# Column maxima of k: from the third batch on by 32x32 transposes on VectorE and a row through DRAM, instead of eight TensorE transposes, with a new order list

## The chip, the cores and the metric

The kernel runs on one core of one Trainium2 chip. The metric is the device time of one execution in microseconds (us). Three runs of the kernel before gave 468.64, 469.94 and 470.07 us; their median is 469.94 us.

## The reference

Two blocks follow each other: linear attention over 8 batches, 8 heads, 576 positions and head size 64, and a feed-forward block (512 to 1024 to 512) over the 4608 rows that come out of it.

```
q_s = softmax(q) over the head size;  k_s = softmax(k) over the 576 positions
kv  = einsum('bhsd,bhse->bhde', k_s, v);  attn = einsum('bhsd,bhde->bhse', q_s, kv)
x   = attn, as (8*576) rows of 8*64
h   = x @ w_in
sm  = softmax(h) over the 1024;  solu = h * sm
ln  = (solu - mean) / sqrt(var + 1e-6) * g_ln
out = ln @ w_out
```

The softmax of k needs, for each of the 512 columns (head, head size) of a batch, the maximum over its 576 positions. The change is about that maximum.

## The kernel before

**Tiles.** The 4608 rows are cut into 36 row tiles of 128 rows: four per batch and, for every pair of batches, a fifth from the 64 rows that each has left over. A row tile goes through `attend` (x, 16 or 32 small matmuls on TensorE, called PE in the profile), `hidden` (h, 24 matmuls of 128x512 and then the chain of SoLU and layer norm on VectorE, ScalarE and GpSimd: DVE, ACT and POOL) and `project` (o, 24 matmuls of 128x512, one eviction, one store). The operands are split in two float16 parts, and h and o are sums of three products each. The transposed u (uT) is made by a DMA transpose, and up to 12 of these tiles stand ready ahead of o.

**Keys.** `keys(b)` (line 354) works once per batch. k lies as 128 partitions by (8 heads, 4 positions, 64), plus the rest of 64 partitions. VectorE takes maxima over the positions within a partition (khalf, ktop; L365, L367) and of the rest (L370). `ktop` is then 128 partitions by 512 columns, and the maximum over the partitions is missing. `tops_of` (line 336) makes it: four PE transposes of 128x128 (`turned`, L341), a maximum on VectorE (`col`, L344), four more PE transposes of the broadcast `col` (`wide`, L348), which puts the 512 maxima on every partition, and a copy out of PSUM on ScalarE (`kb`, L351). Then follow the subtraction from k (`km`, L376, in two halves of four heads, and `kr`, L381), the exponentials (L378, L383), the product with v on PE (`kv`, L395 and L400), the denominators, a power-of-two scale and the block-diagonal `bd` that x reads.

**Queues.** All DMAs are issued by SyncE (SP): loads of q, k, v and the weights, the DMA transposes, and the stores. SP, like the other engines, takes its instructions strictly in order; one that waits holds what is behind it.

**Order.** Nothing is scheduled by a tool. Each piece of work is a generator, and the string `ORDER` names which generator takes its next step: `K2` is the next step of keys of batch 2, `h3` of hidden of the fourth row tile, `o0` of project of the first, `P` a filler of four matmuls (`warm_up`, L696), `Q`, `V`, `LK`, `LQ`, `R`, `S`, `w`, `y`, `W`, `Z` the loads, the query softmax, the scales and the weights. A suffix `.v` puts a step that may run on several engines on VectorE. So the string sets the order within every engine and, for many steps, the engine.

**Start.** In the first 73 us the weights are read as 64-bit words, converted on VectorE and ScalarE (L258 to L330), and the first tiles of x and h are made between; o can only begin when `wo` is ready.

Of the kernel before, what the change touches and what calls it, by code (L numbers as in the profile page):

```python
# [8 lines left out]
F32 = mybir.dt.float32  # L9
# [5 lines left out]
ALU = mybir.AluOpType  # L15
AX = mybir.AxisListType

P = 128
# [3 lines left out]
WHOLE = 1  # L22
ORDER = (
# [78 lines left out]
def linear_attention_solu_ffn(ctx: ExitStack, tc: tile.TileContext, q, k, v, w_in, w_out, g_ln, out):  # L102
# [7 lines left out]
    nc = tc.nc  # L110
    B, H, S, D = q.shape
    DM, DF = w_in.shape[0], w_out.shape[0]
    NP = H // 2
# [647 lines left out]
```

## Time and profile before

| | |
|---|---|
| three runs | 468.64, 469.94, 470.07 us |
| profiled execution | 468.76 us, of which the span of the instructions is 467.0 us |
| busy over the span | PE 439.9, DVE 349.9, ACT 282.4, POOL 200.0 us |
| granted PE clock | 0.996 of full speed |
| moved by DMA | 74.99 MB |

Times in the profile count from the start of the span. Busy is the union of an engine's instructions; a matmul's recorded duration includes its way through the array, so that matmuls that follow each other overlap in the records and the distance of their starts, not their duration, is what each costs. L and a number is a line of the kernel before. In the lists of order that are quoted below, lines of the changed kernel stand 23 higher in this part of the code, and a number behind a tile's name tells buffers apart.

### The profile page before, as it was taken

What the parts mean: (1) busy time and instruction counts of PE and PEld (TensorE: products, weight loads), DVE (VectorE), ACT (ScalarE), POOL (GpSimd) and SP (SyncE); (2) the same over time, 40 slices, a digit from 0 to 9 for tenths busy, and PEclk for the clock granted to TensorE, in tenths of its full rate; (3) what the DMA queues carried; (4) which work ended last, traced back from release to release, by engine and by line L of the source; (5) the groups of instructions that cost most, each with busy time, mean ns of one, the idle gap of its engine ahead of it and who ended that gap; (6) DMA issues with size and microseconds to landing.
All of it is one profiled execution on the core that took longest, in us unless ns stands there. A gap on an engine that the chain in (4) does not pass through costs nothing.

```text
span 467.0 us, 8294 instructions
## 1 busy us (share of the span) xinstructions
PE 439.9 (94%) x3142; PEld 221.4 (47%) x3142; DVE 349.9 (75%) x620; ACT 282.4 (60%) x469; POOL 200.0 (43%) x286
## 2 busy tenths in 40 slices
PE   0678889999999999999999999999999999999997
PEld 0334344455546454545454455445545445444445
DVE  4989999998987889879789788668877844633500
ACT  1789899777658657466667448654764454522401
POOL 4123966577159356314665322735364421211200
PEclk9989999999999999999999999999999999999999
DMA  8999989589593997598757973869324673232522
GB/s 251 311 316 303 208 190 214 104 215 207 152 237 72 219 231 159 146 193 212 146 126 210 226 141 63 226 146 201 71 67 46 135 163 54 60 70 71 133 63 67
DMA packets 159240, 74.99 MB, mean 161 GB/s; under 512 B 127840, under 2 KB 152672, under 8 KB 159200
## 3 DMA queue, kind: packets, MB, share of 16 engines
q1 hardware_dynamic: 159200, 74.47, 69.0%
q8 instruction: 24, 0.39, 0.4%
q14 instruction: 16, 0.13, 0.1%
HBM read 36.70 MB, written 9.44 MB: 99 GB/s over the span
## 4 chain that ended last, share of the span: by engine, by line
PE 86%; DVE 6%; POOL 3%; ACT 3%; DMA 1%; issue 1%; SPq 0%; POOLq 0%; ACTq 0%; DVEq 0%
PE o L640 40%; PE h L566 36%; PE x L529 3%; PE kv L395 3%; PE warm_up L696 1%; DMA qm<-in_q_dram 1%; PE kv L400 1%; DVE wi L289 1%; DVE qnmx L443 1%; POOL qm L445 1%; PE turned L341 1%; PE wide L348 1%; DVE iw L262 1%; POOL km L376 1%; DVE km L376 0%
## 5 line engine op out<-in xcount | busy, mean ns | idle before, releaser
L640 PE MATMUL o<-wo,uT 128*128 128x512 f16 (+1 forms) x888 | 197.4, 373 | 0.0
L566 PE MATMUL h<-wi,xT 128*128 128x512 f16 x840 | 193.1, 379 | 2.7 <-ACT e L609 2.3
L640 PEld LDWEIGHTS <-uT 128*128 128x128 f16 x888 | 86.2, 98 | 97.8 <-issue 0.3
L566 PEld LDWEIGHTS <-xT 128*128 128x128 f16 x840 | 81.5, 98 | 98.8 <-issue 3.0
L573 DVE TENSOR_REDUCE top<-h 128x1 f32<-128x1024 f32 x36 | 43.9, 1221 | 24.9 <-PE h L566 24.7
L602 DVE SCALAR_TENSOR_TENSOR u<-h,nmu,u 128x1024 f16<-128x1024 f32 x36 | 46.0, 1277 | 16.7 <-ACT u L600 16.5
L609 ACT ACTIVATE e<-h,nmu 128x1024 f32<-128x1024 f32 x36 | 40.1, 1113 | 22.1 <-DVE u L602 22.1
L595 DVE SCALAR_TENSOR_TENSOR h<-h,ph,e 128x1024 f32<-128x1024 f32 x36 | 46.3, 1287 | 5.5 <-POOL ph L592 4.0
L589 POOL TENSOR_TENSOR p<-pi,mone 128x1 f32<-128x1 f32 x36 | 25.9, 718 | 49.5 <-DVE pi L586 42.7
L600 ACT ACTIVATE u<-h,nmu 128x1024 f16<-128x1024 f32 x36 | 40.0, 1112 | 0.8
L579 ACT ACTIVATE e<-h,nm,hs 128x1024 f32<-128x1024 f32 x31 | 37.2, 1201 | 0.7
L597 ACT ACTIVATE nmu<-s 128x1 f32<-128x1 f32 x36 | 7.3, 202 | 49.4 <-DVE h L595 49.3
L445 POOL TENSOR_TENSOR qm<-qm,qnmx 128x1024 f32<-128x1024 f32 (+1 forms) x14 | 25.7, 1844 | 21.7 <-DVE qnmx L443 14.6
L650 ACT ACTIVATE os<-o,rr 128x512 f32<-128x512 f32 (+1 forms) x23 | 15.3, 667 | 31.1 <-PE o L640 24.4
L622 POOL TENSOR_TENSOR r<-var,mhalf 128x1 f32<-128x1 f32 x36 | 24.2, 675 | 22.5 <-DVE var L619 22.0
L461 POOL TENSOR_TENSOR qhl<-qm,qhl 128x1024 f16<-128x1024 f32 (+1 forms) x11 | 22.5, 2041 | 19.4 <-DVE qhl L163 10.3
L575 ACT ACTIVATE nm<-top,hs 128x1 f32<-128x1 f32 x31 | 9.1, 294 | 35.2 <-DVE top L573 35.0
L456 POOL TENSOR_TENSOR qm<-qm,qrec 128x1024 f32<-128x1024 f32 (+1 forms) x11 | 20.7, 1879 | 19.2 <-DVE qrec L454 19.1
L543 DVE SCALAR_TENSOR_TENSOR xT<-x,xT 128x512 f16<-128x512 f32 x35 | 23.6, 683 | 5.2 <-ACT xT L541 5.1
L586 POOL TENSOR_SCALAR pi<-am 128x1 f32<-128x1 f32 x19 | 7.5, 393 | 41.8 <-DVE am L583 41.1
L443 DVE TENSOR_REDUCE qnmx<-qm 128x16 f32<-128x1024 f32 (+1 forms) x17 | 19.3, 1147 | 6.0 <-DMA qm<-in_q_dram 6.0
L541 ACT ACTIVATE xT<-x 128x512 f16<-128x512 f32 x35 | 20.0, 590 | 5.9 <-PE x L529 5.8
(139 smaller groups left out, 547.4 us busy)
## 6 DMA issues: line engine op xcount, KB each, us to landing
v<-in_v_dram SPq DMA_DIRECT2D x32, 256.0 KB, 3.7
out_dram<-os SPq DMA_DIRECT2D x31, 256.0 KB, 3.4
km<-in_k_dram SPq DMA_DIRECT2D x7, 1024.0 KB, 7.1
qm<-in_q_dram SPq DMA_DIRECT2D x7, 1024.0 KB, 6.8
w_in<-in_moe_w_in_dram SPq DMA_DIRECT2D x8, 512.0 KB, 6.9
w_out<-in_moe_w_out_dram SPq DMA_DIRECT2D x8, 512.0 KB, 5.6
out_dram<-os SPq DMA_DIRECT2D x10, 128.0 KB, 2.7
qm<-in_q_dram SPq DMA_DIRECT2D x2, 512.0 KB, 4.4
```

The lines of the kernel that those rows point to most:

```text
L443: nc.vector.tensor_reduce(shaped(nmx), x, axis=AX.X, op=ALU.max, negate=True)
L445: on(nc.gpsimd).tensor_tensor(x, x, wide(nmx), op=ALU.add)
L566: nc.tensor.matmul(h[:, ns], xT[:, t, kc], wi[:, s, kc, ns], start=(i == 0), stop=(i == len(terms) - 1))
L573: nc.vector.tensor_reduce(top, h, axis=AX.X, op=ALU.max, negate=True)
L579: nc.scalar.activation(e, h, AF.Exp, bias=nm, scale=hs, accum_out=z)
L589: nc.gpsimd.tensor_tensor(p, pi, mone, op=ALU.pow)
L595: nc.vector.scalar_tensor_tensor(h, h, ph, e, op0=ALU.mult, op1=ALU.mult, accum_out=s1)
L600: nc.scalar.activation(u[:, 0], h, AF.Identity, bias=nmu)
L602: nc.vector.scalar_tensor_tensor(u[:, 1], h, nmu, u[:, 0], op0=ALU.add, op1=ALU.subtract)
L609: nc.scalar.activation(e, h, AF.Square, bias=nmu, accum_out=s2)
L622: nc.gpsimd.tensor_tensor(r, var, mhalf, op=ALU.pow)
L640: nc.tensor.matmul(o, uT[:, j, f], wo[:, s, f, cols], start=(f == 0 and j == 0 and s == 0), stop=(f == NF - 1 and j == 1))
```

## The change

From the third batch on (`b >= SPREAD`, with `SPREAD = 2`, so for six of eight batches) `tops_of` goes another way:

- VectorE transposes `ktop` in blocks of 32x32 (`blocks`, L343 of the changed kernel) and takes the maximum over each run of 32 (`part`, 128 partitions by 16; L346).
- One PE transpose turns `part` into 16 partitions by 128 (`turned`, L349), and VectorE takes the maximum over the four groups of 32 (`row`, 16 by 32: the 512 maxima; L352).
- SP stores `row` in a DRAM buffer (`line`, 2 KB; L355), and, once that has landed, loads it back with a broadcast to all 128 partitions (`kb`, 256 KB; L359).

The first two batches keep the path of before. `kb` is what it was for the subtraction that follows. x stays in single tiles of 16 matmuls, as before.

The order list is a new one: nearly every item stands elsewhere, and a number of steps changed their engine. Its first line, before and after:

```
-    "LQ0*2 Q0a*2 LK0*3 Q0b.v Q0c.v Q0a.v Q0b V03 K0.v w3 Q0a w3 K0 Q0a.v Q0a K0*2 Q0b V03 Q0c.v*2 V00 w0 "
+    "LQ0*2 Q0a Q0b Q0a LK0 Q0c LK0 K0 Q0a LK0 Q0b Q0b.v V03 Q0a w3 Q0c K0 w3 K0 V03 V00.v Q0a.v Q0a*2 w0 "
```

The rest of the diff:

```
+SPREAD = 2
...
+    hbm = ctx.enter_context(tc.tile_pool(name="hbm", bufs=1, space=bass.MemoryType.DRAM))
...
     def tops_of(top, b):
 
         flat = top.rearrange("p h d -> p (h d)")
+        if b >= SPREAD:
+            blocks = sb.tile([P, NP * P], F32, name=f"blocks{b}", tag="kb", bufs=1)
+            nc.vector.transpose(blocks, flat)
+            yield
+            part = sm.tile([P, NP * 4], F32, name=f"part{b}", tag="part", bufs=1)
+            nc.vector.tensor_reduce(part, blocks.rearrange("p (i r) -> p i r", r=32), axis=AX.X, op=ALU.max)
+            yield
+            turned = ps.tile([NP * 4, P], F32, name=f"turned{b}", tag="att", bufs=3)
+            nc.tensor.transpose(turned, part, ident)
+            yield
+            row = sm.tile([NP * 4, 32], F32, name=f"row{b}", tag="row", bufs=1)
+            nc.vector.tensor_reduce(row, turned.rearrange("p (g r) -> p r g", r=32), axis=AX.X, op=ALU.max)
+            yield
+            line = hbm.tile([NP * 4, 32], F32, name=f"line{b}", tag="line", bufs=2)
+            nc.sync.dma_start(out=line, in_=row)
+            yield
+            kb = sb.tile([P, H, D], F32, name=f"kb{b}", tag="kb", bufs=1)
+            wide = line.rearrange("i r -> (i r)").unsqueeze(0).broadcast_to([P, NP * P])
+            nc.sync.dma_start(out=kb.rearrange("p h d -> p (h d)"), in_=wide)
+            yield kb
+            return
         turned = ps.tile([P, NP, P], F32, name=f"turned{b}", tag="att", bufs=3)
         for i in range(NP):
             nc.tensor.transpose(turned[:, i], flat[:, i * P : (i + 1) * P], ident)
```

146 rows, old and new, of the table ORDER are left out of this document.

## The prediction

> **What bounds the kernel now.** I read the page first, for the busy times and the chain that ended last.
>
> ```profile
> PE 439.9 (94%) x3142; PEld 221.4 (47%) x3142; DVE 349.9 (75%) x620; ACT 282.4 (60%) x469; POOL 200.0 (43%) x286
> PE 86%; DVE 6%; POOL 3%; ACT 3%; DMA 1%; issue 1%; SPq 0%; POOLq 0%; ACTq 0%; DVEq 0%
> ```
>
> PE carries 86% of the chain, so the question is whether what the change takes from PE is paid back somewhere. Next I cut the span at 73.21 us, where the chain begins to consist of PE alone, and asked for the busy times of that long stretch, for what PE waited for in it, and for three pieces of the chain.
>
> ```profile
> 73.21:463.50 390.29, 390.29 (x2734) 196.02 (x2733) 286.67 (x510) 225.74 (x382) 166.83 (x249) 1.00 0.64 143
> PE h L566 <- ACT e L609: 0.4, 1, 0.4
> 77.68 5.18 PE o L640 x24
> 119.78 1.52 PE x L529 x64
> 190.73 1.87 PE kv L395 x64
> ```
>
> The first row gives the stretch, PE's busy time in it and then PE's weight loads, DVE, ACT and POOL. PE is busy all of 390.3 us, and the only wait that the trace lists for it is one of 0.4 us. A matmul of o or h costs 5.18/24 = 0.216 us, one of x 1.52/64 = 0.024, one of kv 1.87/64 = 0.029. DVE has 390.3 - 286.7 = 103.6 us free there. So from 73 us on, a microsecond of PE work less is a microsecond less of span, as long as nobody makes PE wait.
>
> **What is removed from PE.** A group of four transposes, twice per batch, shows in the timeline of batch 7; beside it stands a single transpose of the same kind.
>
> ```profile
> 330.31 0.59 PE L640 MATMUL o<-wo,uT 128*128 128x512 f16 x2
> 330.75 0.60 PE L341 MATMUL turned<-ident,ktop 128*128 128x128 f32 x4
> 331.18 1.46 PE L640 MATMUL o<-wo,uT 128*128 128x512 f16 x6
> 332.48 0.60 PE L348 MATMUL wide<-ident,col 128*128 128x128 f32 x4
> 332.91 1.24 PE L566 MATMUL h<-wi,xT 128*128 128x512 f16 x5
> ...
> 113.46 0.27 PE L173 MATMUL kv<-ident,mx 128*128 128x128 f32 x1
> 113.57 0.38 PE L566 MATMUL h<-wi,xT 128*128 128x512 f16 x1
> ```
>
> Starts count, not durations: `turned` takes PE from 330.75 to 331.18, 0.43 us, `wide` from 332.48 to 332.91, again 0.43; the single one 113.57 - 113.46 = 0.11. The new path keeps one transpose (bounds 0.11, and 0.27 if nothing overlaps it; I take 0.11, since it stands between matmuls as the single one does). Per batch 0.43 + 0.43 - 0.11 = 0.75, for six batches 4.5 us less; with the upper bound 3.5.
>
> The Trainium skill, page "TensorE: Matmul & The Clock Gate", section "Part 4: PE-mode transpose", puts one transpose at about 275 ns in a kernel's context. The records' 0.27 us agree as a duration, but the starts stand 0.11 apart; charged singly, 48 removed and 6 added would give 42 x 0.275 = 11.6 us instead of 4.5.
>
> The lists of order show the place. In both, PE's rows are at batch 2: before, between o of the third row tile and x; `bd` and `uT` are the stationary operands.
>
> ```order
> L640 LDWEIGHTS uT0_2_780
> L640 MATMUL o0_20_1084<-wo_68,uT0_2_780 128x512
> L348 MATMUL wide2_1118<-ident_86,col2_1114 128x128 x4
> L529 LDWEIGHTS bd1_81
> L529 MATMUL x1_2_1132<-qT1_2_1054,bd1_81 64x128
> ```
>
> After, on PE, between h of the sixth row tile and o of the third:
>
> ```order
> L589 LDWEIGHTS xT1_0_968
> L589 MATMUL h1_0_1022<-wi_69,xT1_0_968 128x512
> L349 MATMUL turned2_1076<-ident_88,part2_1070 16x128
> L663 LDWEIGHTS uT0_2_830
> L663 MATMUL o0_20_1078<-wo_70,uT0_2_830 128x512
> ```
>
> Two visits of four have become one visit of one, and PE waits for DVE once per batch instead of twice.
>
> **What is added to VectorE, and taken from ScalarE.**
>
> ```profile
> L344 DVE TENSOR_REDUCE col<-turned 128x4 f32<-128x512 f32 x8 | 5.5, 688 | 1.8 <-PE turned L341 1.8
> L163 DVE COPY vm<-v 128x512 f32<-128x512 f32 x7 | 2.8, 403 | 0.0
> L365 DVE TENSOR_TENSOR khalf<-km 128x512 f32<-128x512 f32 x16 | 12.1, 754 | 0.1
> L176 DVE TENSOR_REDUCE top_kv<-kv 128x1 f32<-128x128 f32 x8 | 2.3, 286 | 2.3 <-PE kv L173 2.3
> L351 ACT COPY kb<-wide 128x512 f32<-128x512 f32 x8 | 4.7, 585 | 8.1 <-PE wide L348 8.1
> ```
>
> No 32x32 transpose is in the trace. Over 128x512 in float32 a copy takes 0.40 us and a two-operand instruction 0.75; I take 0.69, as the one-operand reduction of that size (an estimate). Then `part` 0.69 and `row` 0.29 come, and `col` 0.69 goes: 0.98 more per batch, 5.9 us in six batches. ACT loses 6 x 0.585 = 3.5. All of it lies beside PE work, in an engine with 103.6 us free: I cost it at nothing. If that cover is gone, it is at most those 5.9 us.
>
> **What is added to SP, and the new wait.** SP before, around the stores of the first two o (`os`), the loads of q and v, and the transposes of u:
>
> ```order
> L484 DMA_TRANSPOSE qT1_2_1054<-qhl1_1_994 128x16x128
> L201 DMA qm2_1092<-in_q_dram 128x8x256
> L653 DMA out_0_dram<-os0_10_1037 128x512
> L653 DMA out_0_dram<-os0_00_949 128x512
> L605 DMA_TRANSPOSE uT1_1_1168<-u1_1_1068 128x16x128
> ```
>
> SP after, at the same stores:
>
> ```order
> L507 DMA_TRANSPOSE qT1_2_1105<-qhl1_1_1003 128x16x128
> L355 DMA line2_1107<-row2_1103 16x32
> L676 DMA out_0_dram<-os0_10_1049 128x512
> L359 DMA kb2_1162<-line2_1107 128x512
> L676 DMA out_0_dram<-os0_00_979 128x512
> L209 DMA v3_1_1168<-in_v_dram 128x2x256
> L628 DMA_TRANSPOSE uT1_1_1183<-u1_1_1113 128x16x128
> ```
>
> The load of `kb` waits on SP until `line` has landed; behind it are a store, a load of v for the next batch, and the transposes of u. All three are needed much later (up to 12 uT stand ready for o), so that SP's wait costs nothing by itself. On DVE the first half of km waits for kb, with xT and u of two row tiles behind it, and seven instructions between `row` and it; on POOL kr waits, with the second half of km and the next q subtraction behind it. What may cost is the round trip. The nearest transfers are the stores of an output tile and the loads of v, 256 KB like `kb`; the answers by source line give their time to landing.
>
> ```profile
> DMA to landing us min/median/max: 1.9/3.3/8.3
> DMA to landing us min/median/max: 2.9/3.7/9.4
> ```
>
> The first row is the output stores (L653), the second the loads of v (L207). Round trip T = 3.3 + 3.7 = 7.0 us, bounds 1.9 + 2.9 = 4.8 and 8.3 + 9.4 = 17.7. What else stands between `turned` and the second half of kv:
>
> ```profile
> L376 POOL TENSOR_TENSOR km<-km,kb 128x1024 f32<-128x1024 f32 x8 | 18.9, 2359 | 1.7 <-ACT kb L351 1.5
> L381 POOL TENSOR_TENSOR kr<-kr,kb 64x512 f32<-64x512 f32 x5 | 6.3, 1265 | 2.6 <-ACT kb L351 2.5
> L378 ACT ACTIVATE km<-km 128x1024 f32<-128x1024 f32 x16 | 16.8, 1052 | 1.9 <-POOL km L376 1.0 <-DVE km L376 0.7
> ```
>
> 0.27 (the transpose) + 0.29 (`row`) + T + 1.27 + 2.36 + 1.05 = 5.2 + T. Its cover in batch 2 is what the new list puts on PE behind `turned`: 24 matmuls of o, 32 of x, 24 of h, 48 x 0.216 + 32 x 0.024 = 11.1 us, and the first half of kv, 0.9. So PE waits when T exceeds 6.8 us. Counted likewise, batches 3 to 7 have 14.2, 14.7, 18.6, 18.6 and 25.5 us, and wait from T = 9.9, 10.4, 14.3, 14.3 and 21.2. At 7.0 only batch 2 waits, 0.2 us; `row` also stands behind a 0.7 us reduction on DVE, and I take 0.5 us (bounds 0, and 2.2 at T = 9).
>
> The Trainium skill, page "DMA: Bandwidth & Descriptors", section "Anatomy of one DMA", gives about 2.0 us per transfer plus its bytes at 436 GB/s, for DMAs issued by GpSimd. That would be an estimated 2.0 + 2.6 = 4.6 us, and a wait of 0 instead of 0.5.
>
> **The start.** Two moves of the new list touch the chain there, whose rows are:
>
> ```profile
> 12.44 1.22 DVE qm L445
> 13.66 0.59 DVE ktop L370
> ...
> 32.49 1.02 PE warm_up L696 x4
> 33.52 0.57 PE x L529 x16
> ```
>
> DVE before, at the first batch's maxima:
>
> ```order
> L365 TENSOR_TENSOR khalf0_117<-km0_103 128x512
> L367 TENSOR_TENSOR ktop0_116<-khalf0_117 128x256
> L445 TENSOR_TENSOR qm0_97<-qm0_97,qnmx0_2_110 128x8x128
> L370 TENSOR_TENSOR ktop0_116<-ktop0_116,kr0_106 64x512
> L450 TENSOR_REDUCE qsum0_1_145<-qm0_97 128x8
> ```
>
> DVE after, there:
>
> ```order
> L388 TENSOR_TENSOR khalf0_113<-km0_107 128x512
> L479 TENSOR_TENSOR qm0_99<-qm0_99,qrec0_0_126 128x8x64
> L390 TENSOR_TENSOR ktop0_112<-khalf0_113 128x256
> L393 TENSOR_TENSOR ktop0_112<-ktop0_112,kr0_116 64x512
> L473 TENSOR_REDUCE qsum0_1_153<-qm0_99 128x8
> ```
>
> The q subtraction (L445) has gone to POOL, 1.22 us off the chain; and of the fillers between the first kv and the first x there are three instead of four, 1.02. Together 2.2 us at most. But later in the start three engines are full:
>
> ```profile
> 50.00:60.00 10.00, 8.50 (x53) 3.90 (x53) 9.59 (x15) 9.36 (x14) 9.37 (x8) 1.00 1.04 211
> ```
>
> (DVE 9.59, ACT 9.36, POOL 9.37 of 10 us, DMA share 1.04.) The list has as much ACT work up to there as before, so a lead gained early is mostly lost. I take 0.8 us less; bounds 2.2 less and 1.0 more.
>
> **The sum.** -4.5 - 0.8 + 0.5 = -4.8 us. The profiled execution was 468.76 us (span 467.0 and 1.76 around it), the median of the runs 469.94; the two differ by 1.2, so I set out from their middle, 469.4: 464.6 us. With all bounds of this case: 469.4 - 4.5 - 2.2 = 462.7, and 469.4 - 3.5 + 1.0 + 2.2 = 469.1.
>
> **The rivals.** A difference within 0.3%, 1.4 us, can hardly be told from no change.
>
> *The round trip ends slower.* kb lands late, and the subtractions, on DVE or POOL, hold h's chain behind them while PE stands at kv. It decides where the waits of batches 2, 3 and 4 eat the 5.3 us and 1.4 more: (T - 6.8) + (T - 9.9) + (T - 10.4) = 6.7, T = 11.3 us. At T = 12.5 the waits are 5.7 + 2.6 + 2.1 = 10.4, the time 469.4 - 5.3 + 10.4 = 474.5 us. For it speaks that single landings of 8.3 and 9.4 us exist; against it the medians, and that both would have to be slow together in several batches. 9 in 100.
>
> *The start gives it back.* The new list reaches the dense stretch 4 us later: 469.4 - 4.5 + 4.0 = 468.9 us, no change. For it speaks that three engines are full from 50 to 60 us, so one step in the wrong place is felt; against it the two moves above, and that of DVE's list one L445 and one L461 of the start have gone to POOL, which is idle early. 13 in 100.
>
> *The start gains more,* 3 us instead of 0.8, if both moves carry through and a wait of h for its buffer shrinks: 469.4 - 4.5 - 3.0 = 461.9 us. 5 in 100.
>
> *Every transpose costs its recorded duration.* Then PE is freed of (48 - 6) x 0.27 = 11.3 us: 469.4 - 11.3 = 458.1 us. The starts of rows L341 and L640 speak against it. 3 in 100. It is the page's 275 ns of the Trainium skill taken as a price; the trace disagrees with that reading.
>
> That the change doesn't do what it says can be left out: PE's list after has one `turned` and no `wide` in each batch from 2 on.
>
> **How the numbers follow.** The forecast, 464.6 us, has the remaining 70 in 100. Faster by over 0.3%: 70 + 5 + 3 = 78; within: 13; slower: 9. The range of 461.5 to 469.1 us holds the forecast with its bounds, the better start and the start that gives it back; 12 in 100, the last rival and the slower one, lie outside.
>
> **What would show it.** Right: L349 once per batch at 0.11 us of PE between its neighbours; DVE busy about as before, ACT some 3 us less; PE's waits after 75 us below 1.5 us, the longest at kv of batch 2, for exponentials of km; the dense stretch beginning near 72 us. Wrong: waits of kv for km in three batches or more; `line` and `kb` above 11 us together; a 32x32 transpose well over 0.75 us; the first o matmul later than 77.7 us; or new waits of h for e or xT in the dense stretch, which would mean that the new list, not the new path, decides.

## The result and the profile after

| | before | after |
|---|---|---|
| median of five runs | 468.76 us (468.35 to 470.07) | 472.84 us (472.40 to 474.83) |
| ratio, 95% interval | | 1.0087 (1.0059 to 1.0114) |
| span of the profiled execution | 467.0 us | 470.8 us |
| granted PE clock | 0.996 | 0.989 |

The change makes the kernel slower by 4.1 us, 0.9%; forecast were 4.8 us less. Here and below, a ratio leaves out runs of over 1.5% above the fastest of the same kernel (four of twelve in E4 and in E7), and a median holds all runs. The page of the changed kernel, busy times and chain:

```profile
PE 440.5 (94%) x3096; PEld 218.4 (46%) x3096; DVE 359.0 (76%) x614; ACT 279.2 (59%) x463; POOL 206.9 (44%) x304
PE 66%; DVE 16%; DMA 7%; ACT 5%; issue 3%; POOL 1%; SPq 0%; ACTq 0%; DVEq 0%; POOLq 0%
```

PE's busy time is as before although it has work less, and only 66% of the chain are PE's (86% before). What PE waited for from 73 us on, in us in total, times and longest:

```profile
PE h L589 <- ACT e L632: 2.1, 3, 1.1
PE kv L418 <- ACT km L401: 2.1, 1, 2.1
PE o L663 <- ACT os L673: 1.9, 1, 1.9
PE x L552 <- DMA qT<-qhl: 0.3, 1, 0.3
```

Before, this list had one row of 0.4 us. The operations of the new path itself cost what was forecast; by group (busy, mean ns of one) and, for its two DMAs, by issue (KB, median us to landing):

```profile
L343 DVE STREAM_TRANSPOSE blocks<-ktop 128x512 f32<-128x512 f32 x6 | 4.2, 702 | 0.1
L346 DVE TENSOR_REDUCE part<-blocks 128x16 f32<-128x512 f32 x6 | 4.1, 683 | 0.1
L352 DVE TENSOR_REDUCE row<-turned 16x32 f32<-16x128 f32 x6 | 1.6, 274 | 3.6 <-PE turned L349 3.6
L349 PE MATMUL turned<-ident,part 128*16 128x128 f32 x6 | 1.6, 272 | 0.0
```

```profile
kb<-line SPq DMA_DIRECT2D x6, 256.0 KB, 3.9
line<-row SPq DMA_DIRECT2D x6, 2.0 KB, 2.1
```

The 32x32 transpose takes 0.70 us (forecast 0.69), the round trip 2.1 + 3.9 = 6.0 us (forecast 7.0). These are medians: from the issue of `line` to the landing of `kb` it is 5.2 us in batch 2, 8.5 and 8.7 in batches 3 and 4, and 5.0 to 6.8 in the others; of these six, only batch 2 has a kv that waits. So the loss is not in the path's own rows.

**Where PE stands.** The timeline of PE at the first two o (start, us, what; in brackets the idle time before it and its releaser), of before:

```profile
73.21 4.48 PE L566 MATMUL h<-wi,xT 128*128 128x512 f16 x20 [0.41 <-ACT e L609]
77.52 5.34 PE L640 MATMUL o<-wo,uT 128*128 128x512 f16 x24
82.70 1.03 PE L566 MATMUL h<-wi,xT 128*128 128x512 f16 x4
83.70 4.48 PE L640 MATMUL o<-wo,uT 128*128 128x512 f16 x20
```

And of after:

```profile
73.40 5.34 PE L589 MATMUL h<-wi,xT 128*128 128x512 f16 x24 [0.49 <-ACT e L632]
78.57 5.34 PE L663 MATMUL o<-wo,uT 128*128 128x512 f16 x24
85.79 2.53 PE L663 MATMUL o<-wo,uT 128*128 128x512 f16 x11 [1.88 <-ACT os L673]
```

The first o starts 1.05 us later. Of this, 4 x 0.216 = 0.86 us is work that has only changed places: all 24 matmuls of an h stand ahead of the first o now, where before 20 stood ahead of it and four behind. That h itself begins 0.19 us later. So the new list has the second o directly behind the first, and nothing between them. There is one PSUM buffer of o, and ScalarE empties it only after a u, part of q and an xT: PE waits 1.88 us.

The timeline of after at batch 2, all engines:

```profile
102.34 1.28 DVE L618 SCALAR_TENSOR_TENSOR h<-h,ph,e 128x1024 f32<-128x1024 f32 x1
102.39 1.27 POOL L404 TENSOR_TENSOR kr<-kr,kb 64x512 f32<-64x512 f32 x1
...
103.54 5.37 DVE L399 TENSOR_TENSOR km<-km,kb 128x1024 f32<-128x1024 f32 x1
103.62 2.34 POOL L399 TENSOR_TENSOR km<-km,kb 128x1024 f32<-128x1024 f32 x1
...
105.93 1.89 POOL L468 TENSOR_TENSOR qm<-qm,qnmx 128x1024 f32<-128x1024 f32 x1
...
108.94 1.06 ACT L401 ACTIVATE km<-km 128x1024 f32<-128x1024 f32 x1 [3.88 <-DVE km L399]
...
110.05 2.17 PE L418 MATMUL kv<-vm,km 128*64 128x65 f32 x38 [2.05 <-ACT km L401]
```

kb is there at 102.39, for POOL has begun to subtract it. DVE's half of km takes 5.37 us, 1.21 elsewhere: it begins at 103.54 and ends 1.1 us after POOL's string of kr, km and qm. POOL's own half of km is done at 105.96, in time for kv. The product h (L618), whose first operand lies in PSUM, ran beside kr in its usual 1.28. So PE gets the exponentials of DVE's half 2.05 us late. Right behind, the granted clock falls (0.66, the column after POOL's):

```profile
110.00:115.00 5.00, 4.95 (x84) 4.39 (x85) 3.85 (x9) 4.97 (x8) 2.65 (x5) 0.66 0.63 115
```

5 x 0.34 = 1.7 us of PE work more. The same picture stands at the seventh kv (batch 6), with a factor of one element per partition:

```profile
283.31 1.26 POOL L404 TENSOR_TENSOR kr<-kr,kb 64x512 f32<-64x512 f32 x1
283.38 4.05 DVE L615 TENSOR_TENSOR ph<-p,hs 128x1 f32<-128x1 f32 x1 [0.57 <-POOL p L612]
284.54 0.54 POOL L645 TENSOR_TENSOR r<-var,mhalf 128x1 f32<-128x1 f32 x1
285.05 2.35 POOL L399 TENSOR_TENSOR km<-km,kb 128x1024 f32<-128x1024 f32 x1
...
287.53 1.29 DVE L618 SCALAR_TENSOR_TENSOR h<-h,ph,e 128x1024 f32<-128x1024 f32 x1
...
295.46 1.89 PE L589 MATMUL h<-wi,xT 128*128 128x512 f16 x8 [1.08 <-ACT e L632]
```

`ph` takes 4.05 us instead of 0.15, and PE waits for this chain's e at 295 and again (0.58) at 314 us. Take for every DVE record what it lasts beyond the median of the same operation, tile and shape in the kernel before: the sum is 7.6 us before (the longest 1.3) and 15.9 after, 8.1 of it in these two rows.

The Trainium skill, page "SBUF — State Buffer", section "Who interferes with whom", has the rule: a VectorE instruction with two operands in SBUF reads the second through a port that it shares with GpSimd; against a GpSimd instruction that reads SBUF, whoever issues first has it for the whole instruction, and the other is blocked. The two rows agree, and go further: VectorE did not get in between POOL's instructions either, but waited for up to three of them (kr, km, qm).

### The profile page after: what moved, and what is told of

It reads as the page before. It is cut to its first block, busy times and chain, and to the rows that moved or that the text cites. A ratio compares the mean times of both kernels' runs of the same rounds, so it can differ in the third digit from the quotient of the medians.

```text
span 470.8 us, 8231 instructions
## 1 busy us (share of the span) xinstructions
PE 440.5 (94%) x3096; PEld 218.4 (46%) x3096; DVE 359.0 (76%) x614; ACT 279.2 (59%) x463; POOL 206.9 (44%) x304
## 4 chain that ended last, share of the span: by engine, by line
PE 66%; DVE 16%; DMA 7%; ACT 5%; issue 3%; POOL 1%; SPq 0%; ACTq 0%; DVEq 0%; POOLq 0%
PE o L663 32%; PE h L589 29%; DMA km<-in_k_dram 4%; DMA qT<-qhl 3%; PE x L552 2%; PE kv L418 2%; DVE h L618 2%; DVE u L625 2%; DVE km L399 2%; DVE top L596 1%; DVE ph L615 1%; DVE wo L332 1%; DVE gw L264 1%; DVE qsum L473 1%; ACT e L632 1%
## 5 line engine op out<-in xcount | busy, mean ns | idle before, releaser
L618 DVE SCALAR_TENSOR_TENSOR h<-h,ph,e 128x1024 f32<-128x1024 f32 x36 | 46.3, 1286 | 4.3 <-POOL ph L615 3.3
L612 POOL TENSOR_TENSOR p<-pi,mone 128x1 f32<-128x1 f32 x36 | 24.6, 684 | 34.7 <-DVE pi L609 33.1
L484 POOL TENSOR_TENSOR qhl<-qm,qhl 128x1024 f16<-128x1024 f32 (+1 forms) x12 | 24.8, 2067 | 23.2 <-ACT qhl L163 10.5
L606 POOL TENSOR_SCALAR am<-nm 128x1 f32<-128x1 f32 x19 | 8.4, 444 | 56.3 <-ACT nm L598 56.2
L468 POOL TENSOR_TENSOR qm<-qm,qnmx 128x1024 f32<-128x1024 f32 (+1 forms) x13 | 24.7, 1908 | 16.3 <-DVE qnmx L466 16.3
L671 DVE TENSOR_SCALAR os<-o,rr 128x512 f32<-128x512 f32 (+1 forms) x13 | 9.5, 727 | 27.1 <-PE o L663 26.9
L479 POOL TENSOR_TENSOR qm<-qm,qrec 128x1024 f32<-128x1024 f32 (+1 forms) x14 | 26.0, 1855 | 7.3 <-DVE qrec L477 5.8
L609 POOL TENSOR_SCALAR pi<-am 128x1 f32<-128x1 f32 x22 | 6.2, 283 | 45.8 <-DVE am L606 44.6
```

The source lines that it names most:

```text
L468: on(nc.gpsimd).tensor_tensor(x, x, wide(nmx), op=ALU.add)
L479: on(nc.gpsimd).tensor_tensor(x, x, wide(rec), op=ALU.mult)
L484: on(nc.gpsimd).tensor_tensor(lo, x, hi, op=ALU.subtract)
L612: nc.gpsimd.tensor_tensor(p, pi, mone, op=ALU.pow)
L618: nc.vector.scalar_tensor_tensor(h, h, ph, e, op0=ALU.mult, op1=ALU.mult, accum_out=s1)
```

## The experiments

Two theories. **Places:** the path is good for its 4.5 us, and the new list loses more than that by where it puts o, km, kr and ph. **Round trip:** the way through DRAM brings kb too late. As a ruler I take, from PE's timeline, the start of the first o, the time from there to the end of the last matmul, PE's waits of over 0.25 us in between, and the rest without them:

| kernel | median us | ratio to before (95%) | first o | from it to the end | waits | rest |
|---|---|---|---|---|---|---|
| before | 468.76 | | 77.52 | 385.98 | 0 | 385.98 |
| after | 472.84 | 1.0087 (1.0059 to 1.0114) | 78.57 | 388.86 | 5.89 | 382.97 |
| E1 km2_dve | 470.72 | 1.0047 (1.0025 to 1.0068) | 79.56 | 386.36 | 4.79 | 381.57 |
| E2 km2_pool | 470.81 | 1.0058 (1.0028 to 1.0088) | 78.21 | 386.16 | 4.58 | 381.58 |
| E3 ph17 | 474.38 | 1.0120 (1.0089 to 1.0151) | 80.04 | 389.37 | 6.21 | 383.16 |
| E4 o1_att | 471.67 | 1.0024 (0.9995 to 1.0052) | 81.24 | 383.45 | 2.04 | 381.41 |
| E5 order_only | 477.54 | 1.0182 (1.0154 to 1.0210) | 78.85 | 393.19 | 6.66 | 386.53 |
| E6 ph21 | 472.79 | 1.0095 (1.0063 to 1.0127) | 78.51 | 387.29 | 4.58 | 382.71 |
| E7 att_ph21 | 470.84 | 0.9995 (0.9963 to 1.0028) | 82.70 | 386.13 | 3.48 | 382.65 |
| E8 att_ph21_dve | 467.56 | 0.9971 (0.9949 to 0.9994) | 82.03 | 382.42 | 0.94 | 381.48 |
| E9 start_before | 475.21 | 1.0135 (1.0118 to 1.0153) | 77.36 | 393.32 | 6.96 | 386.36 |
| E10 start_before_3 | 467.75 | 0.9980 (0.9962 to 0.9998) | 78.24 | 384.96 | 2.81 | 382.15 |
| E11 hop3 | 476.14 | 1.0122 (1.0078 to 1.0166) | 84.37 | 387.95 | 5.60 | 382.35 |
| E12 upto_k2 | 472.18 | 1.0076 (1.0062 to 1.0090) | 77.10 | 387.92 | 3.82 | 384.10 |
| E13 cover | 469.60 | 1.0022 (1.0005 to 1.0039) | 76.50 | 386.35 | 2.82 | 383.53 |
| E14 cover_os | 470.65 | 1.0034 (1.0014 to 1.0053) | 78.26 | 388.06 | 2.84 | 385.22 |

Each ratio is to runs of the kernel before that were timed beside that kernel; their medians lie between 468.7 and 469.4 us. The four columns behind the ratio are of one execution.

Two things in the rest column have to be taken off before kernels are compared. By the granted clock, a lower clock behind a wait costs 1.7 us in the changed kernel, E3, E6, E7, E12 and E13, 3.4 in E14, 5.1 in E9 and nothing in the others. And before, E12, E13 and E14 have the four matmuls of h (0.86 us) behind the first o that all others have ahead of it. Without both, the rest is 385.1 us before, 386.5 in E5, which has the old path, and 380.9 to 382.4 in the fourteen kernels with the new path, the changed one among them.

E1 to E4 have a list two lines shorter, so their lines stand 2 lower than in the changed kernel; in E11 those behind L355 stand 3 higher. In the diffs of the list, every item is the next step of its generator.

### One repair each (E1 to E4)

E1, batch 2: kr and the second half of km on VectorE.

```
-  ... h6.v K2 K2 K2.v h6.v K2 Q2a ...
+  ... h6.v K2 K2.v K2.v h6.v K2.v Q2a ...
```

> Only batch 2: kr and the second half of km go from POOL to VectorE; all else is the changed kernel. Held (DVE's subtraction, both operands in SBUF, cannot run while POOL works through its string of such instructions): no POOL string stands beside the first half of km any more, so that instruction drops from 5.37 us to between 1.2 us and 2.0 us (only the q subtraction of POOL, 1.9 us, can still hold it), and PE's wait of 2.1 us at kv of batch 2 goes; with the higher clock after it the span falls from 470.8 by 2 to 3.5 us, to 467.3 to 468.8. Round trip (kb comes too late by way of DRAM): nothing changes in when kb lands, so the wait at kv stays within 0.5 us of 2.1, or grows, since DVE now does three subtractions in a row (3.2 us) behind the same landing; span 470.8 or more.

```profile
103.36 1.90 POOL L466 TENSOR_TENSOR qm<-qm,qnmx 128x1024 f32<-128x1024 f32 x1
104.51 1.83 DVE L397 TENSOR_TENSOR km<-km,kb 128x1024 f32<-128x1024 f32 x1
...
108.91 1.15 PE L416 MATMUL kv<-vm,km 128*64 128x65 f32 x32
111.01 1.15 PE L416 MATMUL kv<-vm,km 128*64 128x65 f32 x32 [0.95 <-ACT km L399]
```

As Places said: km takes 1.83 us, held only by POOL's qm; the first half of kv no longer waits, the clock stays at 1.00 behind it. The second half waits 0.95 us for three subtractions in a row. The span, 469.3 us, is above the 467.3 to 468.8 expected: in this execution the first o came 1 us later than in the changed kernel's.

E2, the other way round: the first half of km on POOL too.

```
-  ... h6 K2.v h4.v ...
+  ... h6 K2 h4.v ...
```

> The other way round, batch 2 only: the first half of km goes from VectorE to POOL as well, so that all three subtractions stand on POOL. Held: POOL takes 2.35 us for what DVE does alone in 1.2, but nothing is held; the first half ends near 104.8 us instead of 108.9, kv's first half no longer waits; the second half of km ends near 108.5 and its exponential near 109.6, so PE waits 0.5 to 1 us at the second half of kv instead of 2.1 at the first. Span 468.5 to 470. Round trip: POOL starts its string of 6 us when kb lands and the wait at kv becomes longer than 2.1 us; span 471 to 473. In short, the slower engine is the faster choice only if the two engines stand in each other's way.

All three on POOL, each at half of DVE's speed, and PE waits 0.59 us at the second half of kv instead of 2.05 at the first; the span is 467.8, below the 468.5 to 470 expected. The slower engine makes PE wait less here, because nobody is held. The round-trip theory expected the wait to stay or grow in E1 and E2; it fell in both, so for this wait that theory is out. The medians are 2.1 and 2.0 us below the changed kernel's, but the intervals of the ratios overlap with its interval: it is the waits in the traces that show the effect.

E3, a `ph` of batch 5 from VectorE to POOL.

```
-  ... K5 h18.v K5 h17.v h15 ...
+  ... K5 h18.v h17 K5 h15 ...
```

> Batch 5 only: the factor ph of one row tile (one element per partition) goes from VectorE to POOL, one place ahead of kr. Held: ph takes 0.2 to 0.4 us on POOL instead of the 4.05 us in which DVE was held behind POOL's kr, r and km; the chain of that tile ends 3.5 us earlier, and PE's waits of 1.08 and 0.58 us for e near 295 and 314 us shrink to under 0.6 in sum; kr and km on POOL start 0.3 later. Span 469 to 470. The rival (these waits come from the order of the tiles, which stand too close in the new list, and ph is only busy while something else is late): the waits stay within 0.4 us of 1.66 in sum, span 470.4 to 471.2.

A miss of mine: the row at 283 us belongs to batch 6, so the edit touched another instruction, and `ph` still took 4.04 us there. It shows the scatter instead: with batch 2 untouched, kv waited 2.60 us there, and the median was 1.5 us above that of the changed kernel.

E4, another PSUM buffer for the second o.

```
-            o_tag = "att" if t >= LATE and (t + i) % 2 else "o"
+            o_tag = "att" if t == 1 or t >= LATE and (t + i) % 2 else "o"
```

> Only the second o gets another PSUM buffer (the tag of x and kv, of which three stand), so that it need not wait for ScalarE to copy the first o out. List and path are unchanged. If the wait of 1.9 us before the second o is a cost of the place that the new list gave it: the wait goes, PE runs through from 78.6 us on, and the span falls by 1.5 to 2.2 us, to 468.6 to 469.3. The rival: PE gets to batch 2 earlier by 1.9 us, while the subtractions there are set by kb and by DVE and POOL and not by PE, so the gain is waited off at kv of batch 2: its wait grows from 2.1 to 3.5 us or more, and the span stays at 470.3 to 471.

The wait of 1.88 went, and the one at kv of batch 2 almost too (0.26), though nothing was changed there. The timeline shows why:

```profile
104.17 1.22 DVE L397 TENSOR_TENSOR km<-km,kb 128x1024 f32<-128x1024 f32 x1
...
104.17 2.35 POOL L402 TENSOR_TENSOR kr<-kr,kb 64x512 f32<-64x512 f32 x1 [1.11 <-PE o L661]
```

Both subtractions start in the same instant by the records, DVE's takes its usual time, and POOL's kr was held (2.35 instead of 1.27). The span, 468.1, is even below the 468.6 to 469.3 expected, but the twelve runs lie between 467.3 and 476.3 us.

### The list alone, and repairs together (E5 to E8)

E5, the new list with the old path in all batches.

```
-SPREAD = 2
+SPREAD = 8
-  ... h4.v*2 K2.v K2 h4.v K2 o2.v ...
+  ... h4.v*3 K2 o2.v ...
```

(and likewise in batches 3 to 7).

> The new list with the old way to kb in all eight batches: the four transposes stand where the new path has its one, wide stands where the store of line stood, the copy on ScalarE where kb was loaded; the two VectorE steps of the new path are left out. Everything else keeps its place. List: the places that the new list gave to o, km, kr and ph cost the time, and the path itself saves its 4.5 us of PE; then this kernel is slower than the changed one, by 4.5 us less what the missing round trip frees at kv of batch 2 (2 to 3.7 us): 473.5 to 477 us, and the waits before the second o (1.9 us) and for e near 295 us stay. Path: the detour through DRAM costs the time; then this kernel is as fast as the one before, 467.5 to 470 us.

```profile
103.41 1.27 POOL L404 TENSOR_TENSOR kr<-kr,kb 64x512 f32<-64x512 f32 x1
...
104.73 5.19 DVE L399 TENSOR_TENSOR km<-km,kb 128x1024 f32<-128x1024 f32 x1
...
111.06 1.15 PE L418 MATMUL kv<-vm,km 128*64 128x65 f32 x32 [1.69 <-ACT km L401]
```

477.54 us: the list alone costs some 8 us, and the path gives back 1.0182 - 1.0087 = 0.0095 of 469, 4.5 us, with some 2 us of uncertainty. That it is the forecast 4.5 is partly luck: between the two profiled executions the rest without the clock differs by 5.3, the waits and the start together by about 1, and the changed kernel loses 1.7 to the clock. The time is 0.5 above the range I had set, since nothing was freed at kv (1.69 + 0.31 us of waits there). The hold of km is there too, without any round trip: kb came from ScalarE. That settles it between the two theories for the changed kernel.

E6, the right `ph`, of batch 6, on POOL ahead of kr.

```
-  ... K6 x24 h21 K6 h21.v h23.v ...
+  ... K6 x24 h21*2 K6 h23.v ...
```

> The factor ph that took 4.05 us on VectorE at 283.4 us belongs to batch 6, not to batch 5: the seventh kv stands at 290.7 us. Here that ph goes to POOL, one place ahead of kr; all else is the changed kernel. Held: ph takes 0.2 to 0.4 us, the product h behind it on VectorE starts 3.5 us earlier, and PE's waits for e near 295 and 314 us (1.08 and 0.58 us) go, or shrink to under 0.6 in sum. From the first o to the end 388.9 us become 387.2 to 388. The rival (the tiles stand too close in the list, whoever is late): the two waits stay within 0.4 us of 1.66 in sum.

```profile
283.68 0.19 POOL L615 TENSOR_TENSOR ph<-p,hs 128x1 f32<-128x1 f32 x1
283.83 1.26 POOL L404 TENSOR_TENSOR kr<-kr,kb 64x512 f32<-64x512 f32 x1
...
283.90 1.29 DVE L618 SCALAR_TENSOR_TENSOR h<-h,ph,e 128x1024 f32<-128x1024 f32 x1 [0.84 <-POOL ph L615]
```

0.19 instead of 4.05 us, h 3.6 earlier, and both waits for e are gone (from 1.66 us to none over 0.25). From the first o to the end it is 387.29 us, inside the 387.2 to 388 expected. The median did not follow, 472.79: kv of batch 2, untouched, waited 2.44 in the profiled execution.

E7, the second o's buffer and this `ph`, the edits of E4 and E6.

> The two repairs together: the other PSUM buffer for the second o, and ph of batch 6 on POOL ahead of kr. If each wait is a cost of its own and they add: from the first o to the end 383.5 us (with the buffer alone) become 382 to 382.8, since at most 0.3 us at kv of batch 2 and 0.4 us for the transposed q are left of PE's waits after the start; the median falls to 466.5 to 469 us, a ratio to the kernel before of 0.995 to 1.000, the spread of the start's runs included. If the waits only move: the sum of PE's waits after the first o stays above 1.5 us.

Its runs spread from 465.4 to 475.0 us. In the profiled one, with 474.0 near the upper end, the balance of batch 2 had tipped the other way:

```profile
105.53 1.26 POOL L404 TENSOR_TENSOR kr<-kr,kb 64x512 f32<-64x512 f32 x1 [1.01 <-PE o L663]
...
105.63 6.40 DVE L399 TENSOR_TENSOR km<-km,kb 128x1024 f32<-128x1024 f32 x1
...
113.17 2.06 PE L418 MATMUL kv<-vm,km 128*64 128x65 f32 x38 [3.08 <-ACT km L401]
```

The instructions in this place are E4's, but POOL was 0.10 us ahead: DVE is held for 5.2 us, and PE waits 3.08 instead of 0.26. The expected 382 to 382.8 us from the first o to the end were missed (386.13), and the waits, 3.48 us, are above the 1.5 that I had set as the sign that waits only move. That this tipping makes the spread of the runs is argued from one profile each of E4 and E7.

E8, the edits of E1, E4 and E6 together.

> As the run with the two repairs, and in batch 2 kr and the second half of km on VectorE as well. There the first half of km took 1.2 us with the buffer alone, because kb came when VectorE and POOL were both free; which of the two starts first is a matter of tenths of a microsecond. With all three on VectorE it cannot tip over: PE's wait at kv of batch 2 is 0.3 to 1 us at the second half, for three subtractions in a row, and the runs lie closer together than with the two repairs alone. If the tipping does not matter, this kernel is 0 to 0.7 us slower than the one with two repairs and spreads as widely (467 to 476 us with the buffer alone).

```profile
PE kv L418 <- ACT km L401: 0.9, 1, 0.9
PE h L589 <- ACT e L632: 0.6, 1, 0.6
PE x L552 <- DMA qT<-qhl: 0.2, 1, 0.2
```

With nothing left to tip over in batch 2, the twelve runs lie between 466.3 and 470.0 us, and the kernel is the fastest of all: 0.9971 (0.9949 to 0.9994), 1.4 us. The rest, 381.48, is 3.6 us less than before's for the same work. In the profiled execution, with 469.65 us one of the slower of the twelve, the late start (first o at 82.03, 3.7 us later at the same work) takes all of that back; when the other eleven have their first o is not on record.

### The start, and a longer trip (E9 to E11)

E9, the items up to the first o from the list of before, then the changed list; E10, the same with the three repairs. The seam, where the bar stands:

```
 ... h2 Z*2 | h5.v Z o0 o0.v h2 h2.v h3.v V22 R1.v h3 Z h3 o0 ...
```

> The items up to the first o are taken from the list of the kernel before, all that is then left in the order of the changed list; the new path, the waits after the start and everything else are those of the changed kernel. If the new list's start costs 1.05 us and more where it tips (first o at 78.6 instead of 77.5 us, 81 to 83 in three of the profiles): first o at 77.3 to 78.3 us, the waits behind it as in the changed kernel, span 469 to 470, ratio to the kernel before 1.003 to 1.007. If the start is not to blame (the first o moves with the chip, not with the list): nothing changes, ratio 1.008 to 1.012.

> The start of the kernel before, and behind it the three repairs together (the second o's buffer, ph of batch 6 on POOL, km and kr of batch 2 on VectorE). If all costs are found and add: first o at 77.3 to 78.3 us, from there to the end 382.4 us as with the three repairs, so a span of 463.2 to 464.2 and a time of 465 to 466 us, ratio to the kernel before 0.990 to 0.994; that is the 4.5 us of the path, less about a microsecond of waits. If the start's lateness is the chip's: ratio 0.995 to 0.999, as with the three repairs alone (0.997).

The first o came at 77.36 and 78.24. But the gain was lost at the seam: in E9 the second o waits 3.15 us instead of 1.88 and kv 2.05 and 0.32, and the lower clock behind the two long waits costs 5.1 us; in E10 an h waits 1.43 for the e of an earlier tile. E9's ratio lies above both ranges that I had set, E10's within E8's interval; the 465 to 466 us expected of E10 were missed.

E11, E8 with one more copy within DRAM.

```
+            hop = hbm.tile([NP * 4, 32], F32, name=f"hop{b}", tag="hop", bufs=2)
+            nc.sync.dma_start(out=hop, in_=line)
+            line = hop
             kb = sb.tile([P, H, D], F32, name=f"kb{b}", tag="kb", bufs=1)
```

> The three repairs, and the row of maxima makes one more copy within DRAM before it is broadcast, in all six batches: the round trip, 6.0 us, grows by some 2 us, to 7.5 to 8.5. By the cover that the prediction counted (PE waits from 6.8, 9.9, 10.4, 14.3, 14.3 and 21.2 us on) only batch 2 can feel it: its wait at kv grows from 0.9 to between 1.7 and 3.2 us, kv of the other five batches waits nowhere over 0.3 us, and the time rises by 0.8 to 2.5 us (4 if the clock dips behind the wait), to a ratio of 0.999 to 1.005. If the round trip were what the change suffers from, three batches or more wait at kv, and the time rises by more than 4 us, above a ratio of 1.006.

```profile
kb<-hop SPq DMA_DIRECT2D x6, 256.0 KB, 3.8
line<-row SPq DMA_DIRECT2D x6, 2.0 KB, 2.3
hop<-line SPq DMA_DIRECT2D x6, 2.0 KB, 2.0
```

The three medians make 8.1 us, and kv waits 2.12 us in batch 2, 0.76 in batch 3 and 0.40 in batch 4. From the issue of `line` to the landing of `kb` these three trips are 8.1, 10.2 and 10.7 us: above the 6.8, 9.9 and 10.4 from which the prediction had them wait. So its count of the cover is right to half a microsecond for batches 3 and 4; what I missed is that the trip is not the same in every batch. A further wait shows what is queued behind a waiting instruction on DVE: in batch 5 the first half of km stands 2.48 us there for kb, the eviction of an o stands behind it, and PE waits 1.82 us for that. Three batches wait and the ratio is 1.0122: that is what I had set down as the round-trip theory's sign. Against E8's profile it has 4.7 us more of waits and a start 2.3 later (84.37, the latest of all). So a trip that is 2 us longer does hurt, and there is little to spare; with the trip as it is, E8 waits 0.94 us at kv.

### Less seam (E12 to E14)

E12, the list of before up to the maxima of batch 2, then the changed list with E1's and E6's repairs. The list at the seam:

```
 ... K2.v h5.v h4.v K2.v K2 R1.v h4.v o2 K2 LQ2 h4.v o1.v h4 V32 V20 o2 K2.v K2 o2.v x6 ...
```

> The list of the kernel before up to the maxima of batch 2 (some 95 us, so also the places of the first two o, without the other buffer), behind it the rest in the order of the changed list with ph of batch 6 on POOL and km and kr of batch 2 on VectorE; the new path in batches 2 to 7. Where the lists meet, the last maximum, the 32x32 transpose, part, turned, row and line of batch 2 are put a few items earlier. If the path is good for its 4.5 us and the places of the new list were the loss: first o at 77.3 to 78.3 us, from there to the end 386.0 us (before) less 4.5, plus 0.3 to 2 us of waits (kv of batch 2, the seam), so 381.8 to 383.5, span 462.5 to 465.2, ratio 0.989 to 0.996. If the start's spread and the granted clock take it back as with the start of before spliced in further ahead: ratio 0.996 to 1.000.

```profile
104.58 1.23 DVE L399 TENSOR_TENSOR km<-km,kb 128x1024 f32<-128x1024 f32 x1 [3.08 <-DMA kb<-line]
...
106.95 1.15 PE L418 MATMUL kv<-vm,km 128*64 128x65 f32 x32 [1.46 <-ACT km L401]
110.46 1.15 PE L418 MATMUL kv<-vm,km 128*64 128x65 f32 x32 [2.36 <-ACT km L401]
```

Here the round trip was late: `line` took 3.8 and kb 4.4 us, 8.2 in all, against 1.3 and 3.8 in the changed kernel's batch 2, and `turned` stands closer to kv than in the changed list (10.6 instead of 11.9 us of PE work between them). Why the transfers were slower was not tried. Time and ratio, 472.18 us and 1.0076, lie above everything that I had expected. E13 puts 18 matmuls of the fourth o ahead of that kv, E14 also gives the copy of that o to VectorE:

```
-  ... h3 h6 x7 h6 h4 h4.v h6.v K2 K2.v ... h4.v K2.v o2 K2.v h4.v h3.v ...
+  ... h3 h3.v h6 x7 h6 h4 h4.v h6.v o2 K2 o3 K2.v ... h4.v o3.v*2 o3 K2.v*2 h4.v ...
```

```
-  ... K2 o3.v h6 Q2c K2.v K2 Q2a h7.v h6 o3 ...
+  ... K2 o3.v*2 h6 Q2c K2.v K2 Q2a h7.v h6 ...
```

> The kernel with the list of before up to the maxima of batch 2, in which PE waited 1.46 and 2.36 us at kv of batch 2 (line and kb took 3.8 and 4.4 us there, 8.2 instead of 6.0), with 18 matmuls of the fourth o (3.9 us) put ahead of that kv, and what they need of POOL and ScalarE with them; else the same. If the round trip's cover in batch 2 is all that was left: both waits go, or shrink to under 0.6 us in sum, no other of PE's waits after the start is over 0.5 us, from the first o (77.1 us) to the end 382 to 383.5 us, span 462.5 to 464.5, ratio to the kernel before 0.989 to 0.995. If the wait is passed on (kv later, so bd, x and h of batch 2 later, or uT of the fourth o not there): waits of 1.5 us or more stand elsewhere before 140 us, and the ratio stays above 1.000.

> As the kernel with more cover, where both waits at kv of batch 2 went, but a new one of 2.82 us stood at 120.92: the fifth o waited for ScalarE to copy the fourth out of the one buffer of o, which was third in a row there. Here VectorE makes that copy, directly behind the fourth o; the rest is the same. If each of these waits is a cost of the place and not of the path: this one goes, the clock does not dip behind it (1.7 us in the run before), and from the first o to the end 386.3 us become 381.8 to 383, against 386.0 of the kernel before; span 461.8 to 463.5, ratio 0.987 to 0.993. If it is passed on again: waits of 1.5 us or more before 140 us, and a ratio above 0.997.

The waits at kv went, and each time another came, of E13 first and of E14 behind it:

```profile
120.92 4.34 PE L663 MATMUL o<-wo,uT 128*128 128x512 f16 x12 [2.82 <-ACT os L673]
```

```profile
125.52 0.39 PE L552 MATMUL x<-qT,bd 128*64 128x128 f16 x3 [2.35 <-DMA qT<-qhl]
```

None of these is for km or kb any more. From 140 us on, PE has no wait of over 0.25 us in E12 to E14; but a list mended at one place by hand passed its wait on to the next, and I did not get the whole 4.5 us into a time: E13 and E14 are 0.2% and 0.3% slower than before.

## Why the prediction was wrong, point by point

- *PE bounds, and the transposes give 4.5 us.* Right. By the distances of their starts, behind the first o the 48 transposes take 5.3 us of PE before and the six 0.65 after, 4.7 less. The rest, at the same work and without the clock, agrees more loosely: the fourteen kernels with the new path have 381.4 in the middle, 3.7 less than before (385.1) and 5.1 less than E5 (386.5).
- *DVE's new work is hidden, at nothing.* Right for the new instructions, each within 0.02 us of its estimate. **The step that failed is the one behind it:** "What may cost is the round trip". I named what is queued behind the waiting instructions on DVE and POOL, and priced none for standing in each other's way. The sum 5.2 + T follows POOL's kr and its half of km alone; with T as measured in batch 2, 5.2 us, it gives no wait, and that half was indeed ready in time. DVE's half, which has no term in the sum, ended last: 5.37 us instead of 1.21, held by POOL's string. The wait of kv in batch 2, the right place by luck, was 2.05 instead of 0.5, and not from the round trip.
- *The round trip.* T = 7.0 was 6.0 in the median, and in E5 the wait was there without it. The rival by which it ends slower is not what happened; E11 shows that it comes true with a trip that is 2 us longer.
- *The start, -0.8.* The first o came 1.05 later, at 78.57, where I had written that later than 77.7 would show me wrong. But 0.86 of it is the four matmuls of h, moved and not added; the start itself is +0.2, so that the 0.8 was not gained, and little was lost. With the start of before (E9, E10, E12 to E14) the first o comes at 76.5 to 78.3, with the new one and one buffer of o (the changed kernel, E1 to E3, E5, E6) at 78.2 to 80.0; at the same work the two ranges overlap, so that the list makes it later by more than this is not shown.
- *Nobody makes PE wait in the dense stretch.* That held for the list of before, and I carried it over to a new one of which I had counted the work ahead of each kv, and not what else stands side by side. It costs 1.88 (second o), 1.08 + 0.58 (ph of batch 6) and 0.30 us.

The sum as measured: -3.9 (path, with all else that the rest holds) + 0.2 (start) + 1.88 + 2.05 + 1.66 + 0.30 (waits) + 1.7 (the clock behind the longest) = +3.9; the spans differ by 3.8. The first term is what is left of the rest, and not measured by itself. The path was sound, and the list decided, as the last sentence of the prediction's test has it; it had a rival at the start alone (13 in 100), and none in the dense stretch.

Open: why the first o comes 2.5 to 6 us later than in the changed kernel in the profiles of all four kernels with the new start and the other buffer (E4, E7, E8, E11; E10, with the other buffer and the start of before, has it at 78.24). Up to 85 us their lists are the changed kernel's; in each, PE waits 2.1 us ahead of 24 matmuls of h at 54 us, these take 7.03 us instead of 5.34, at a lower granted clock, and then one conversion of a weight on DVE takes 2.2 instead of 0.7 us beside POOL. Whether that is chance was not settled.

## What to carry to other kernels

When a change comes with a new order, read the whole order: for each engine pair that can block one another, which long instructions of the one stand beside a string of the other, and for each single buffer, whether its two users stand back to back. Where an instruction with two operands in SBUF can run on either engine, try it on the one on which its neighbours in time run, even if that engine is slower: at kv of batch 2 it made 0.59 us of a wait of 2.05 (E2). And run the new order with the old path: that one kernel told more than any repair.

## What the runs showed of the hardware

- DVE is held not for one instruction of POOL but for a string: 5.37, 5.19 and 6.40 us where the instruction alone takes 1.21, and 4.05 for one of 0.15. Which of the two is held was decided by 0.1 us (E4 and E7). POOL is held likewise: kr 2.35 instead of 1.27.
- The granted clock fell (0.66 over 5 us in the changed kernel, 1.7 us of work) behind nine of the ten waits of PE of over 2 us after the first o, and behind none of those up to 1.9 us; the tenth is E11's, of 2.12 us. If the one makes the other, a wait of 2 us costs nearly four; these traces only show them side by side, and no run was made to test it.
